# A split-mask attention and maxout FFN kernel: the program rewritten as one list of commands, with the engine of each mask and copy, the place of each FFN unit and the whole order set by an offline search

One core of one Trainium2 chip. The metric is device time in microseconds (us), the median of several executions. One execution of each kernel was also profiled; its span is from the first to the last instruction, some 2 us less than the time.

## The reference

Attention over 4 batches of 8 heads, 768 positions of 64 values, then a feed-forward layer (FFN) with three input weights and a maximum in place of an activation. Cut to what matters:

```python
causal = rel >= 0
stream_keep = causal & (is_sink | in_win)            # 4 sinks, a window of 64
mask = np.where(retrieval_head, causal, stream_keep) # per head
a = softmax(where(mask, q @ k.T / 8, -1e9))
x = (a @ v) -> (3072, 512)
h = max(max(x @ w1, x @ w2), x @ w3)                 # 512 -> 768
return h @ w_out                                     # 768 -> 512, float32
```

## The kernel before

Attention goes in 16 tiles `t`: batch, half of the positions, four heads. A tile's scores are made in two or four units `u`; ScalarE (ACT) takes the exponential of a unit from PSUM into `pt`; a mask multiplies part of `pt` in place; TensorE (PE) multiplies it with v (`av`); VectorE (DVE) divides by the row sums, giving `x`. When all of a half batch's `x` is turned, its FFN block is queued: 18 units of four products, then three output tiles of six products. FFN units fill PE's time between score units. In the timelines shown below DVE starts its instructions in the order of the program, so that one which waits holds up those behind it (run e4 further down has 19.2 us of such waiting).

The order comes out of a table: each row has the number of FFN units beside one score unit and four strings of other commands. Masks and copies follow fixed rules.

```python
MASK_ON_DVE = ((2, 0, 1), (3, 0, 0), (3, 0, 1), (3, 1, 3), (5, 0, 0), ...)   # 10 instructions
def masks(t, i, u):                      # right behind the scores of (t, u)
    ...
    engine = nc.vector if (t, i, u) in MASK_ON_DVE else nc.gpsimd
    engine.tensor_tensor(out=x, in0=x, in1=m, op=ALU.mult)
# in ffn():
    if wi == 0:
        acc[ni] = accp.tile([P, HALF], FP16, tag="acc", name="acc")
        nc.scalar.copy(out=acc[ni], in_=yy[:, 0:HALF])        # always ACT
    else:
        nc.vector.tensor_tensor(out=dst, in0=yy[:, 0:HALF], in1=acc[ni], op=ALU.max)
    yield
...
PROGRAM = (
    (2.4, True, "", "", "cast 1 2 dp", ""),        # 2.4 FFN units beside scores (2, 0)
    (1.6, True, "", "av 2 0", "", "turn 1 0 0 0"),
    ...
```

The softmax here doesn't subtract the row's maximum and nothing guards it: scores larger than these inputs give would overflow.

Of the kernel before, what the change touches and what calls it, by code (L numbers as in the profile page):

```python
# [38 lines left out]
APART = [(0, 0, 1, (384,), 128, 0), (1, 1, 1, (384,), 128, 0)] + MASKED[1][1:]  # L39

# [11 lines left out]
def kernel(  # L52
# [14 lines left out]
    nc = tc.nc  # L67
# [21 lines left out]
    BY_DMA = (2, 4, 5, 6, 7, 8, 9, 10, 11, 12, 13, 14, 15)  # L89

    consts = ctx.enter_context(tc.tile_pool(name="consts", bufs=1))
    stage = ctx.enter_context(tc.tile_pool(name="stage", bufs=3))
    half16 = ctx.enter_context(tc.tile_pool(name="half16", bufs=3))
# [27 lines left out]
    def load_pairs(half, hp, n, engines, alone=False):  # L121
        for nm, src, eng in zip(("ks", "qs"), (k, q), engines):
            st = stage.tile([P, 4, HB, D], FP32, tag=nm, name=nm)
            m = 2 if alone else 2 * n
            for h in range(0, 2 * n, m):
                eng.dma_start(
                    out=st[:, h : h + m],
                    in_=src[
                        0, 2 * hp + h : 2 * hp + h + m, half * HALF : (half + 1) * HALF
                    ].rearrange("h (p j) d -> p h j d", p=P),  # L130
                )
            for i in range(n):
                staged.setdefault((half, hp + i), []).append(st[:, 2 * i : 2 * i + 2])

# [12 lines left out]
    def turn_pair(half, hp, *engines):  # L147
# [4 lines left out]
        for part, op in enumerate(engines):  # L152
            tr = bank([P, 1024], FP16, "tr")
            for i in range(n):
                for j in range(HB):
                    c = i * HALF + j * P
                    nc.tensor.transpose(  # L157
                        tr[:, c : c + P],
                        xs[part + i][:, j].rearrange("p h d -> p (h d)"),
                        ident,  # L160
                    )
# [34 lines left out]
    after = consts.tile([1, 2], FP16, name="after")  # L196

    def sync_after(x):
        nc.sync.dma_start(out=after, in_=x)
# [3 lines left out]
    def load_v(b, half, engines=None):  # L203
        engines = engines or (nc.sync,) * HB
        vs = stage.tile([P, H, HB, D], FP32, tag="vs", name="vs")
        for j in range(HB):
            r0 = half * HALF + j * P
            engines[j].dma_start(
                out=vs[:, :, j], in_=v[b, :, r0 : r0 + P].rearrange("h p d -> p h d")
            )  # L210
        staged_v[b, half] = vs

    load_pairs(0, 0, 1, (nc.sync, nc.scalar))
    ir32 = consts.tile([1, 2 * H], mybir.dt.int32, name="ir32")
    nc.sync.dma_start(out=ir32, in_=is_retrieval.bitcast(mybir.dt.int32).unsqueeze(0))
    load_pairs(0, 1, 1, (nc.sync, nc.scalar))
    load_pairs(0, 2, 2, (nc.sync, nc.scalar), True)
    load_v(0, 0)


    zero = consts.tile([P, 512], FP16, name="zero")
    nc.vector.memset(zero, 0.0)

# [52 lines left out]
    def head_flags():  # L276
        flags = bank([P, H], FP32, "flags")
        nc.tensor.matmul(flags, base[0:1, 0:P], RT1, start=True, stop=True)
# [26 lines left out]
    def load_weight(wi):  # L305
        if wi < 3:
            nc.gpsimd.dma_start(
                out=w_t[wi],
                in_=(moe_w1, moe_w2, moe_w3)[wi].rearrange("(ks p) n -> p ks n", p=P),
            )  # L310
        else:
            nc.gpsimd.dma_start(
                out=woutt, in_=moe_w_out.rearrange("(ns p) m -> p ns m", p=P)
            )
# [4 lines left out]
    def ffn(b, half):  # L319
# [15 lines left out]
        for wi, ni in order:  # L335
            yy = psum()
            for ks in range(KS):
# [5 lines left out]
                )  # L343
            if wi == 0:
                acc[ni] = accp.tile([P, HALF], FP16, tag="acc", name="acc")
                nc.scalar.copy(out=acc[ni], in_=yy[:, 0:HALF])  # L346
# [6 lines left out]
        for tb in range(HB):  # L353
# [5 lines left out]
            for c, op, eng in (  # L359
                (0, nc.scalar.copy, nc.sync), (n, nc.vector.tensor_copy, nc.scalar),  # L360
# [14 lines left out]
    queue = []  # L375

    def fill(n):
# [28 lines left out]
    def scores(t, u, pairs=(0, 1)):  # L406
# [5 lines left out]
        m = 1 if u == 1 and (t == 0 or t == 1 and pairs == (0,)) else 2  # L412
# [37 lines left out]
        for x, st in sts.items():  # L450
# [5 lines left out]
            if not early:  # L456
                masks(t, i, u)


    MASK_ON_DVE = ((2, 0, 1), (3, 0, 0), (3, 0, 1), (3, 1, 3), (5, 0, 0), (5, 1, 0), (5, 1, 1), (7, 0, 1))  # L460

    def masks(t, i, u):
# [3 lines left out]
        for at, u0, nu, cols, n, m0 in APART if t in (3,) else MASKED[half]:  # L466
# [11 lines left out]
            engine = nc.vector if (t, i, u) in MASK_ON_DVE else nc.gpsimd  # L478
# [4 lines left out]
    def av(t, i):  # L483
# [29 lines left out]
        if t in BY_DMA:  # L513
# [6 lines left out]
    def turn_x(t, i, op=None):  # L520
        b, half, qd = where(t)
        hp = 2 * qd + i
        if t not in BY_DMA:
# [10 lines left out]
        if hp == NHP - 1:  # L534
# [4 lines left out]
    cast_pair(0, 0, (act, act))  # L539
    idle_work(8)  # L540
    read_flags()
    idle_work(2)
    head_flags()
    turn_pair(0, 0, dve, act)
    head_masks(0, True)
    cast_pair(0, 1, (pool, act))
    turn_pair(0, 1, dve)
    cast_pair(0, 2, (pool, pool))
    scores(0, 0, (0,))
    scores(0, 1, (0,))  # L550
    head_masks(1, True)
    load_weight(0)
    scores(0, 0, (1,))
    far_flags()
    cast_pair(0, 3, (pool, pool))
    head_masks(3, True)
    head_masks(2, True)
    turn_pair(0, 2, dve)
    scores(0, 1, (1,))
    turn_pair(0, 3, dve)  # L560
    prep_v(0, 0, dve, nc.gpsimd)
    prep_v(1, 0, dve, nc.vector)
    load_pairs(1, 0, 2, (nc.gpsimd, nc.gpsimd))
    prep_v(1, 1, pool, nc.gpsimd)
    scores(1, 0, (0,))
    scores(1, 1, (0,))
    scores(1, 0, (1,))
    prep_v(0, 1, act, nc.vector)
    av(0, 0)
    scores(1, 1, (1,))  # L570
    av(1, 0)
    av(0, 1)
    turn_x(0, 0, act)
    av(1, 1)
    load_weight(1)
    turn_x(0, 1, act)
    head_masks(0)
    cast_pair(1, 1, (act, act))
    load_pairs(1, 2, 2, (nc.gpsimd, nc.gpsimd))
    load_weight(2)  # L580
    load_v(0, 1, (nc.gpsimd,) * HB)
    turn_x(1, 0, dve)
    turn_x(1, 1, dve)
    cast_pair(1, 0, (act, act))
    fill(4)
    head_masks(2)
    turn_pair(1, 1, dve)
    turn_pair(1, 0, dve)
    head_masks(3)
    load_weight(3)  # L590
    fill(1)
    fill(1)
    fill(1)
    head_masks(1)






    FIRST = 4
    PROGRAM = (
        (2.4, True, "", "", "cast 1 2 dp", ""),
        (2.4, False, "load 1 0", "", "cast 1 3 da", ""),
        (2.0, False, "", "pair 1 2", "load 1 1", ""),
        (2.2, False, "pair 1 3", "v 2 0 ap", "", "v 2 1 ap"),
        (2.2, False, "", "gate, load_v 1 0", "", ""),
        (1.6, True, "", "av 2 0", "", "turn 1 0 0 0"),
        (1.0, True, "turn 1 0 0 1", "", "av 2 1, turn 1 0 1 0", ""),
        (2.2, True, "turn 1 0 1 1, load_v 1 1", "", "v 3 1 pp, v 3 0 ap, x 2 0", "turn 1 1 0 0"),  # L610
        (3.6, False, "turn 1 1 0 1", "x 2 1", "turn 1 1 1 1, av 3 1", ""),
        (2.8, False, "v 4 0 pp, av 3 0", "turn 1 1 1 0", "v 4 1 ap", ""),
        (3.6, False, "x 3 0, x 3 1", "", "", ""),
        (3.6, False, "av 4 0", "", "x 4 0, v 5 1 pp", "x 4 1, v 5 0 ap"),
        (2.8, False, "", "", "av 4 1", "av 5 0, load 2 0, v 6 0 pp"),
        (3.6, False, "x 5 0", "load 2 1", "", "av 5 1"),
        (3.8, False, "", "x 5 1", "", ""),
        (2.8, False, "", "load_v 2 0", "turn 2 0 1 0", "v 6 1 ap"),
        (4.8, False, "turn 2 0 0 1", "", "turn 2 0 0 0", "av 6 0"),
        (4.2, False, "", "", "", "x 6 0, x 6 1, turn 2 0 1 1"),  # L620
        (3.4, False, "", "av 6 1", "turn 2 1 0 1", ""),
        (5.4, False, "load_v 2 1", "v 7 0 ap, turn 2 1 0 0", "turn 2 1 1 0", "v 7 1 ap"),
        (3.4, False, "", "turn 2 1 1 1", "v 8 0 ap, x 7 0", "av 7 0"),
        (3.8, False, "av 7 1", "", "", "v 8 1 pp"),
        (3.94, False, "x 7 1", "", "av 8 0", "v 9 0 ap, av 8 1"),
        (3.2, False, "", "x 8 0, x 8 1", "", ""),
        (3.94, False, "", "", "av 9 0, v 9 1 ap", "load 3 0"),
        (3.6, False, "", "x 9 0, load 3 1", "x 9 1", ""),
        (5.6, False, "v 10 0 ap, av 9 1", "v 10 1 ap", "", ""),
        (3.14, False, "", "load_v 3 0", "turn 3 0 1 0", ""),  # L630
        (3.6, False, "turn 3 0 0 1", "av 10 0", "turn 3 0 0 0", ""),
        (3.4, False, "", "x 10 0", "av 10 1", "turn 3 0 1 1"),
        (6.2, False, "", "", "turn 3 1 0 1", "v 11 0 ap"),
        (3.2, False, "load_v 3 1", "turn 3 1 0 0", "turn 3 1 1 0", ""),
        (3.2, False, "v 11 1 pp", "x 10 1, turn 3 1 1 1", "v 12 0 ap", "av 11 0, x 11 0"),
        (3.4, False, "", "av 11 1", "", "v 12 1 ap"),
        (5.0, False, "x 11 1", "", "av 12 0", "v 13 0 ap, av 12 1"),
        (3.2, False, "", "x 12 0, x 12 1", "", ""),
        (4.0, False, "", "", "av 13 0, v 13 1 pp", ""),
        (5.2, False, "", "x 13 0", "x 13 1", ""),  # L640
# [86 lines left out]
```

## Time and profile before

| | before |
|---|---|
| time, median of 3 runs | 200.88 us (200.74 to 201.45) |
| span, mean TensorE clock | 199.3 us, 0.998 |
| busy: PE, DVE, ACT, POOL (GpSimd) | 95%, 61%, 66%, 62% |
| PE waits of over 0.1 us | 5.5 us, the last at 49.5 us |
| first FFN product, second block's first | 17.79 us, 50.08 us |

Here PE's share, 95% against 66% for the next, says what sets the time, and the place of its waits says where time can be won. Waits here and below are the gaps ahead of an instruction in the timeline of the engine, each with the instruction that ended it.

### The profile page before, as it was taken

The page shows a single profiled execution, that of the slowest core. Times are in us where ns is not written, and L with a number is a line of the kernel's source. Part 1 is how long each engine was busy: PE and PEld are TensorE (multiplying, and loading weights), DVE is VectorE, ACT ScalarE, POOL GpSimd, SP SyncE. Part 2 cuts the span into 40 slices and gives each one's busy share as a digit, 9 for nine tenths or more (in the row PEclk, how much of TensorE's full clock was granted, in tenths as well). Part 3 has the DMA queues.
Part 4 walks back from the last instruction along what each step waited for, and adds up shares of the span by engine and source line. Part 5 has one row for each costly group of instructions (what it writes and reads, how often), then busy time and mean ns, then how long its engine had stood idle before and what let it go on. Part 6 is the DMA issues. An engine that isn't in the chain of part 4 may idle for free.

```text
span 199.3 us, 5133 instructions
## 1 busy us (share of the span) xinstructions
PE 189.7 (95%) x2059; PEld 109.5 (55%) x2059; DVE 122.5 (61%) x241; ACT 131.7 (66%) x206; POOL 123.3 (62%) x154
## 2 busy tenths in 40 slices
PE   7897999996999999999999999999999999999992
PEld 2455555545566465574555565565555565755652
DVE  2698587999687829861555649961555234543540
ACT  4585798786966776676786775848758769323221
POOL 3599159789887906787969635799847447400000
PEclk9999999999999999999999999999999999999999
DMA  6999999994949991904359995513410250023004
GB/s 182 270 213 245 278 238 212 213 202 112 256 81 154 194 274 43 178 0 146 95 101 132 170 254 141 85 26 98 116 23 20 105 76 20 3 64 135 3 0 158
DMA packets 43245, 26.48 MB, mean 133 GB/s; under 512 B 33558, under 2 KB 38230, under 8 KB 43222
## 3 DMA queue, kind: packets, MB, share of 16 engines
q1 hardware_dynamic: 37206, 15.01, 34.9%
q0 software_dynamic: 4784, 10.23, 26.7%
q10 hardware_dynamic: 1232, 0.92, 1.5%
q8 instruction: 16, 0.26, 0.6%
q14 instruction: 7, 0.06, 0.1%
HBM read 25.17 MB, written 6.29 MB: 158 GB/s over the span
## 4 chain that ended last, share of the span: by engine, by line
PE 78%; DVE 8%; ACT 4%; DMA 3%; issue 3%; POOL 2%; SPq 1%; ACTq 0%; POOLq 0%; DVEq 0%
PE yy L338 43%; PE yy L364 12%; PE st L441 10%; PE oacc L495 8%; DVE KQ L190 4%; PE yst L338 3%; ACT pt L452 3%; DMA ks<-in_k_dram 2%; DVE x L505 2%; DMA out_dram<-ot 1%; PE tr L157 1%; PE yst L364 1%; POOL kn L139 1%; DVE hT L349 1%; POOL qn L139 0%
## 5 line engine op out<-in xcount | busy, mean ns | idle before, releaser
L479 POOL TENSOR_TENSOR pt<-pt,mk 128x512 f16<-128x512 f16 (+1 forms) x76 | 80.6, 1084 | 34.8 <-ACT pt L452 34.7
L452 ACT ACTIVATE pt<-st 128x1024 f16<-128x1024 f32 (+3 forms) x99 | 83.1, 894 | 19.4 <-PE st L441 18.6
L349 DVE TENSOR_TENSOR acc<-yy,acc 128x384 f16<-128x384 f32 x45 | 25.1, 558 | 28.9 <-PE yy L338 19.3
L338 PE MATMUL yy<-xT,w1t 128*128 128x384 f16 x180 | 36.1, 327 | 0.1
L338 PE MATMUL yy<-xT,w0t 128*128 128x384 f16 x180 | 35.6, 326 | 0.4 <-DVE xT L531 0.4
L338 PE MATMUL yy<-xT,w2t 128*128 128x384 f16 x180 | 35.7, 327 | 0.0
L346 ACT CAST acc<-yy 128x384 f16<-128x384 f32 x45 | 21.0, 485 | 17.0 <-PE yy L338 10.5
L364 PE MATMUL yy<-woutt,hT 128*128 128x512 f16 (+1 forms) x138 | 32.0, 375 | 0.0
L441 PE MATMUL st<-KQ 32*128 32x384 f16 (+4 forms) x560 | 28.7, 279 | 1.0 <-DVE KQ L190 0.8
L349 DVE TENSOR_TENSOR hT<-yy,acc 128x384 f16<-128x384 f32 x45 | 25.1, 560 | 6.6 <-PE yy L338 4.0
L495 PEld LDWEIGHTS <-pt 128*128 128x128 f16 x672 | 24.0, 97 | 5.3 <-issue 2.1
L190 DVE STREAM_TRANSPOSE KQ<-kq 128x384 f32<-128x384 f32 x24 | 25.7, 1130 | 0.0
L338 PEld LDWEIGHTS <-w0t 128*128 128x128 f16 x192 | 18.2, 98 | 12.9 <-issue 1.0
L495 PE MATMUL oacc<-va,pt 128*128 128x65 f16 x352 | 24.8, 193 | 0.3 <-ACT va L392 0.3
L338 PEld LDWEIGHTS <-w2t 128*128 128x128 f16 x192 | 17.6, 98 | 13.3 <-issue 2.1
L338 PEld LDWEIGHTS <-w1t 128*128 128x128 f16 x192 | 17.2, 98 | 12.8 <-issue 1.3
L370 ACT COPY ot<-yy 128x512 f32<-128x512 f32 x22 | 12.9, 588 | 15.9 <-PE yy L364 9.6
L364 PEld LDWEIGHTS <-hT 128*128 128x128 f16 x150 | 14.0, 98 | 14.6 <-issue 0.3
L441 PEld LDWEIGHTS <-KQ 32*128 32x128 f16 (+1 forms) x560 | 12.2, 93 | 17.8 <-issue 11.5
L495 PE MATMUL oacc<-vf,pt 128*128 128x65 f16 x320 | 21.2, 193 | 0.8 <-POOL vf L394 0.8
L505 DVE TENSOR_TENSOR x<-oacc,rc 128x384 f16<-128x384 f32 x32 | 17.8, 557 | 1.1
L503 DVE RECIPROCAL rc<-oacc 128x6 f32<-128x6 f32 x32 | 6.1, 192 | 20.0 <-PE oacc L495 19.8
(70 smaller groups left out, 129.9 us busy)
## 6 DMA issues: line engine op xcount, KB each, us to landing
out_dram<-ot SPq DMA_DIRECT2D x23, 256.0 KB, 3.1
vs<-in_v_dram SPq DMA_DIRECT2D x21, 256.0 KB, 6.3
kq<-in_k_dram POOLq DMA_DIRECT2D x6, 384.0 KB, 5.6
kq<-in_q_dram POOLq DMA_DIRECT2D x6, 384.0 KB, 8.0
qs<-in_q_dram ACTq DMA_DIRECT2D x4, 192.0 KB, 4.0
ks<-in_k_dram SPq DMA_DIRECT2D x4, 192.0 KB, 3.6
w0t<-in_moe_w_dram POOLq DMA_DIRECT2D x1, 768.0 KB, 7.4
ks<-in_k_dram POOLq DMA_DIRECT2D x2, 384.0 KB, 7.2
```

Source lines behind the costliest of these rows:

```text
L190: nc.vector.transpose(out=dst.rearrange("c (p j) -> c j p", j=n)[:, j0:j1], in_=src.rearrange("c (j i) -> c j i", i=R),)
L338: nc.tensor.matmul(yy[:, 0:HALF], w_t[wi][:, ks, ni * P : (ni + 1) * P], xT[b, half][ks].rearrange("p a t -> p (a t)"), start=(ks == 0), s ...
L346: nc.scalar.copy(out=acc[ni], in_=yy[:, 0:HALF])
L349: nc.vector.tensor_tensor(out=dst, in0=yy[:, 0:HALF], in1=acc[ni], op=ALU.max)
L364: nc.tensor.matmul(yo[:, 0:n], hT[ns][:, tb * P : (tb + 1) * P], woutt[:, ns, c : c + n], start=(ns == 0), stop=(ns == NNB - 1),)
L370: op(out=ot[:, c : c + n], in_=yo[:, 0:n])
L441: nc.tensor.matmul(sts[g // m][:, g % m, c0 : c0 + n * P], KQ[rows, 0, ki * P : (ki + 1) * P], KQ[rows, 1, t0 : t0 + n * P], start=(c0 == ...
L452: nc.scalar.activation(out=pts[t, i][:, u, h0 : h0 + m, 0:w], in_=st[:, :, 0:w], func=AF.Exp, scale=sc,)
L479: engine.tensor_tensor(out=x, in0=x, in1=m, op=ALU.mult)
L495: nc.tensor.matmul(o[:, qi, hl, 0 : D + 1], pt[:, u, hl, c : c + P], vv[:, 2 * hp + hl, ki, 0 : D + 1], start=(idx == 0), stop=(idx == len ...
L503: nc.vector.reciprocal(out=rc, in_=o[:, :, :, D])
L505: nc.vector.tensor_tensor(out=x, in0=o[:, :, :, 0:D], in1=rc.unsqueeze(3).to_broadcast([P, HB, 2, D]), op=ALU.mult,)
```

## The change

The table and the rules are replaced by one list of commands, run from left to right. Each mask (`k tile pair unit engine`), FFN unit (`f 1 engine`, the engine being that of its copy out of PSUM), cast and turn is an entry. An offline search set the order and engines. The intent is to remove the waits that rules and a table cannot avoid. The commands used here: `s` scores and exponential, `k` mask, `v` prepares v, `av` product with v and division (with `D` a DMA turns the result), `x` turns a result on PE, `turn` turns q or k on DVE, `cast`/`turnp` do so for the first batch, `load*`, `ld` and `w` issue loads; the rest build masks and flags. Engines: `a` ACT, `d` DVE, `p` POOL.

```diff
-    MASK_ON_DVE = ((2, 0, 1), (3, 0, 0), ...)
-    def masks(t, i, u):
+    def masks(t, i, u, engine):
-                nc.scalar.copy(out=acc[ni], in_=yy[:, 0:HALF])
+                copy_out[0](out=acc[ni], in_=yy[:, 0:HALF])
-    def fill(n):
+    def fill(n, op=nc.scalar.copy):
+        copy_out[0] = op
-    PROGRAM = ((2.4, True, "", "", "cast 1 2 dp", ""), ...)   # 47 rows, and the calls ahead of it
+PROGRAM = (
+    "cast 0 1 ap, idle 8, cast 0 0 aa, cast 0 2 pp, read, idle 2, w 0, flags, em 0, em 2, em 1",
     ... (cut)
+    "x 0 1 d, av 1 0, x 1 0 d, cast 1 1 pa, w 2, x 1 1 a, turnp 1 1 ad, f 1 d, f 1 a, f 1 a",
     ...
+    "v 8 0 pp, f 1 a, f 1 a, av 7 0 D, k 8 0 0 d, k 7 1 1 d, av 7 1 D, x 7 1 d, f 1 d, f 1 a",
     ...
+    "k 10 0 1 p, load 3 1, f 1 a, load_v 3 0, f 1 a, k 10 0 3 p, turn 3 0 0 1, av 10 0 D",
     ...
+    "f 1 a, v 11 1 pp, av 11 1 D, f 1 a, k 12 0 0 d, f 1 a, v 12 0 pp, s 12 1, turn 3 1 1 1",
+    "x 11 1 a, v 12 1 ad, k 12 1 0 d, turn 3 1 1 0, s 13 0, k 13 0 0 p, f 1 d, k 12 0 1 d",
     ...
+    for line in PROGRAM:
+        for item in line.split(", "):
+            name, *args = item.split()
+            do[name](*args)
```

Loads got options that the list hardly uses, and the product that spreads the head flags reads a row of ones of its own.

## The prediction

> **What bounds the kernel now.** I read the busy shares first, then the PE work in stretches, then the waits, the chain, and the groups for durations.
>
> ```profile
> PE 189.7 (95%) x2059; PEld 109.5 (55%) x2059; DVE 122.5 (61%) x241; ACT 131.7 (66%) x206; POOL 123.3 (62%) x154
> DMA  6999999994949991904359995513410250023004
> ```
> TensorE is busy for 95% of the span and nothing else passes 66%, so only 9.6 us of it are idle by this count. The second line shows the DMA engines full for the first 50 us (ten slices of 5 us).
>
> ```profile
> 0.00:10.00 10.00, 7.95 (x43) 3.58 (x43) 4.81 (x20) 4.60 (x9) 4.50 (x15) 1.00 0.93 226
> 10.00:20.00 10.00, 8.62 (x114) 5.43 (x111) 9.29 (x23) 7.14 (x15) 10.00 (x17) 1.00 1.12 229
> 20.00:30.00 10.00, 9.88 (x83) 5.42 (x81) 7.33 (x15) 8.59 (x15) 3.68 (x7) 1.00 1.10 257
> 30.00:40.00 10.00, 9.92 (x122) 5.72 (x120) 8.88 (x14) 8.18 (x11) 8.39 (x10) 1.00 1.14 213
> 40.00:50.00 10.00, 7.79 (x131) 4.52 (x127) 9.76 (x17) 7.53 (x12) 9.61 (x11) 1.00 0.70 155
> 50.00:60.00 10.00, 10.00 (x132) 6.07 (x121) 7.52 (x15) 8.01 (x14) 8.26 (x13) 1.00 0.80 171
> 60.00:80.00 20.00, 20.00 (x233) 11.38 (x232) 14.23 (x25) 14.19 (x20) 12.12 (x12) 1.00 0.94 167
> ```
> Columns: PE, PEld, DVE, ACT, POOL. All idle PE time lies before 50 us and in the tail after the last matmul (about 195.7 to 199.3). From 50 us PE stays full although no other engine is. In 40 to 50 DVE (9.76) and POOL (9.61) are full while PE drops to 7.79.
>
> The chain of waits says why:
> ```profile
> 39.32 1.99 DVE KQ L190 x2
> 41.37 0.56 DVE x L505
> 41.92 1.99 DVE KQ L190 x2
> 43.92 0.25 DVE pt L479
> 44.17 2.94 DVE KQ L190 x3
> ```
> DVE turns the next batch's q and k, eight transposes of about 1 us, before batch 1 can score; the first feed-forward block is used up meanwhile, and the next one's first product runs at 50.08.
>
> **PE work without stalls.** I summed starts to starts, not busy time. From stretches of the chain: four 384-wide products 0.65 us (32 in 5.31), six 512-wide 1.29 (12 in 2.59), 16 score matmuls 0.56, 8 in 0.34 to 0.45, attention-value 0.37 (12) or 0.97 (30), three transposes 0.17. Over the whole program this gives 176 us from the first transpose (5.75) to the last matmul (195.7), 190 us apart: about 14 us of stalls and rounding, some 10 of them before 50.08, where only 34.3 us of work is done in 44.3. After 50 the stalls that I can find add to under 1 us. **So what can be won lies before 50 us, and about 10 us is its ceiling.**
>
> [...]
> - [...] one 384-wide product is drawn as 327 ns but 32 take 5.31 us, 166 ns each. Hence the sums above.
> - [...]
> - [...] the smaller mask on DVE is slower in the mean (1096 ns) than the larger (588 ns), and one lasted 2.31 us.
> - [...]
>
> ```profile
> L479 DVE TENSOR_TENSOR pt<-pt,mk 128x256 f16<-128x256 f16 x4 | 4.4, 1096 | 0.8 <-ACT pt L452 0.8
> L479 DVE TENSOR_TENSOR pt<-pt,mk 128x512 f16<-128x512 f16 x6 | 3.5, 588 | 3.0 <-ACT pt L452 3.0
> L479 POOL TENSOR_TENSOR pt<-pt,mk 128x512 f16<-128x512 f16 x64 | 73.1, 1160 | 34.7 <-ACT pt L452 34.7
> L346 ACT CAST acc<-yy 128x384 f16<-128x384 f32 x45 | 21.0, 485 | 17.0 <-PE yy L338 10.5
> L392 ACT CAST va<-vs 128x384 f16<-128x384 f32 x22 | 11.3, 516 | 0.0
> ```
>
> **The change part by part.** Comparing the order of instructions:
> - PE gets 3 more transposes (one more x pair turned on PE, one fewer by DMA): +0.17 us. Nothing else is added or removed on it.
> - ACT loses 17 acc copies (485 ns), 5 output copies (588), 11 v casts (516) and 3 q/k casts (510), and gains 4 copies of turned q/k and one of x (480 to 800): 8.2 + 2.9 + 5.7 + 1.5 - 2.7 = 15.6 us less, to about 116.
> - DVE takes those 17 (an estimate of 0.56 each, as its 384-wide PSUM operations take) and 5 (0.69, extrapolated from 0.42 for 256 and 0.56 for 384), 8 of the v casts (0.45), 2 q/k casts (0.54), 3 more vf products, and 31 masks instead of 10. The masks cost 0.3 to 0.4 us alone and 0.6 to 1.1 beside POOL. That is 9.5 + 3.5 + 3.6 + 1.1 + 1.6 + 6 to 20, less 2 for copies given to ACT: 23 to 37 us more, to some 145 to 160.
> - POOL loses 21 masks (0.7 to 1.16 us) and gains 3 v casts: about 20 us less, to 103.
>
> Total work is thus not the point, since PE has the same; **the placing is**. I split the new list at the second block's first product and added each engine's work with the durations above, operations back to back, masks on DVE uncontended.
>
> Up to the first product the list holds 7.6 us of PE work. It starts later: ACT casts pair 1's k first, whose load landed only at 5.6 before, so both of pair 0's inputs are ready near 6.9 instead of 5.2 (transposes began at 5.75). The exponentials then end near 16.6 (15.9 before). The fourth x copy stands behind a q cast on ACT that waits for the second half's q; before, ACT's cast of it ended a DMA wait at 19.36. So the first block's first four-matmul product finishes near 19.9, against 19 before. The second weight is now issued behind another 0.79 MB of q and k; at the roughly 250 GB/s that the profile's slices show here this is 3 us, from 23.4 to 25 or 26. PE has its six first-weight products to run till about 25, so this costs little beyond them.
>
> From there to the second block's first product: PE 22.1 us, DVE about 20.5, ACT about 20. Saturated, that product comes at 25.2 + 22.1 = 47.3, against 50.1. With three engines at over 90% and each waiting in order for the others, I add 1 to 2 us: **48.3 to 49.3, a win of 1 to 2 us.**
>
> The next 20.8 us of PE work, which ran without stalls before, now carry 18.7 us of DVE work plus contended masks (seven or so, 0.5 us each, an estimate from the rows above): DVE at about its limit. Loss 0 to 1.5 us.
>
> From there PE has 120.5 us of work and DVE 77: PE bound, as before; the tail is unchanged.
> Sum: 200.88 - 1.5 + 0.7 = 200.1 by my hand sums, 195 if the stalls before 50 us go as the search intended.
>
> **The rivals.**
> 1. *The search works.* It could place every operation and may know landing times better than I do; if the second weight lands by 23.4 and the following work saturates PE, the second block starts at about 45.5 and nothing is lost after: a win of 4.5, to 196.4; with an earlier first product too, 194.5. For it: 10 us of stalls are there, and that DVE and POOL are full from 40 to 50 is just what a finer order can spread. Against: DMA is full for those 50 us.
> 2. *DVE becomes the bound.* With 23 to 37 us more on it, masks slowed by POOL hold up the maxima behind them, and PE waits between 25 and 70 us. Then 200 to 203. For it: the 2.31 us mask. Against: DVE averaged 61%.
> 3. *The prologue waits for loads.* The reordered loads hold the first and second weights' products 2 us longer, nothing wins it back: 200 to 202.
>
> **Range and chances.** A search of all this freedom is seldom spent for nothing, so I weight rival 1 and my hand sum about equally and set 198.0, 80% within 194.3 to 201.4. Over 2% faster means below 196.9: 0.38. Over 2% slower means above 204.9: 0.04. Within: 0.58.
>
> **What would show it.** Right: the second block's first product near 47 to 49 us instead of 50.08; DVE above 72% of the span, ACT below 60%, POOL near 52%; no PE wait after 70 us; PE work unchanged. For rival 1: that product before 46.5 and PE full from 25 us. For rival 2: DVE over 9 in each ten us from 25 to 70, masks on DVE above 0.8 us in the mean, PE waiting for DVE maxima or copies of it. For rival 3: PE idle near 17 to 26 us, released by a weight's DMA or by the ACT copy of x. I am wrong outright if PE stalls after 70 us, or if the first products start well before 18 us.

(Cut from it are remarks that no trace or run of this case shows. No term of its sum is cut: 200.88 - 1.5 + 0.7 = 200.1 stands, and 198.0 is that weighed about equally with rival 1. The author's figures for masks on DVE, 0.3 to 0.4 us alone and 0.6 to 1.1 beside POOL, are rough: in the trace of before the three with POOL idle took 0.28 to 0.43 us, the five with POOL busy throughout 0.46 to 2.31.)

## The result, and the profile after

The changed kernel is correct and **slower by 10%**: 221.9 us (median of 4 runs, 219.59 to 223.15) against 200.91. One of the 4 runs (223.15, clock 0.959) is slow; the fast ones took 219.59 to 222.35. The ratio is 1.0988, 95% interval 1.0923 to 1.1053. Here and below a ratio is that of fast runs alone, so not quite the ratio of the medians quoted, and gains between runs are taken from it, with 1% as 2.0 us: by it the loss is 20 us. The before kernel ran beside every experiment, at 200.86 to 201.42.

From the page of the changed kernel, busy totals and the slices of 5.5 us:

```profile
PE 196.0 (89%) x2062; PEld 111.5 (51%) x2062; DVE 146.0 (66%) x298; ACT 118.6 (54%) x176; POOL 100.7 (46%) x134
...
PE   7695969869799899969999699958999999999993
...
PEclk9889999999999999999999969995899999999999
```

The work moved just as counted beforehand (DVE 146.0, ACT 118.6, POOL 100.7), and PE has three instructions more. But PE's row now has holes up to 155 us, and **the granted TensorE clock, full up to the last microseconds before, drops to 0.50 near 10, 130 and 150 us**.

The stretches that answer to those of before; columns are stretch, length, PE, PEld, DVE, ACT, POOL busy (instructions), clock, DMA share, GB/s:

```profile
10.00:20.00 10.00, 8.30 (x94) 5.06 (x93) 7.66 (x21) 7.34 (x16) 7.48 (x14) 0.87 1.07 250
...
40.00:50.00 10.00, 7.24 (x105) 4.20 (x108) 7.64 (x14) 7.70 (x10) 8.18 (x10) 1.00 0.26 50
50.00:60.00 10.00, 8.44 (x130) 5.10 (x119) 6.81 (x12) 6.28 (x9) 7.02 (x11) 1.00 0.99 238
60.00:80.00 20.00, 18.89 (x207) 10.23 (x205) 19.02 (x37) 12.83 (x19) 10.29 (x14) 1.00 0.67 115
...
120.00:140.00 20.00, 18.09 (x188) 9.46 (x187) 12.38 (x23) 11.53 (x16) 10.45 (x11) 0.91 0.61 132
140.00:160.00 20.00, 16.55 (x163) 8.68 (x162) 11.59 (x24) 7.33 (x12) 5.50 (x8) 0.83 0.11 32
```

From 40 to 50 us *no* engine is full, where DVE and POOL were full before. From 140 to 160 PE works 16.55 of 20 us at a clock of 0.83, and the other engines idle too. Each waits for another, as the timelines below show for one place: a low busy share (DVE's is 11.59 of these 20 us, and it holds PE up for 3.45) does not say that an engine is not in the way.

PE's waits of over 0.1 us add to 20.2 us, 14.7 more than before. Half clock (0.50 granted) adds to that: by the clock of each stretch below full, 8 to 12.5 us lost 1.65 us, 128.1 to 132.1 1.7, 150 to 158 3.0, together 6.4, where before lost 0.4 in all. 14.7 + 6.0 = 20.7, and the spans differ by 220.6 - 199.3 = 21.3. **So in these two profiled executions they hold nearly the whole loss.** The share of the half clock varies between executions of the same program: the fast runs had mean clocks of 0.969 (the profiled one), 0.977 and 0.984, and took 222.35, 221.45 and 219.59 us. The second block's first product comes at 58.09, 8.0 us later than before; the rest is lost behind it. The waits of a microsecond and more behind that point:

| at us | wait | ended by | what the list does there |
|---|---|---|---|
| 76.8 | 1.04 | DVE, the last maximum of a block | a turn and a mask (1.11 us, POOL busy beside it) stand ahead of it on DVE |
| 98.4 | 1.76 | DVE mask `k 7 1 1 d` | stands behind the division of `av 7 0` and the masks of `k 8 0 0 d`, just ahead of its own `av 7 1` |
| 127.1 | 1.75 | POOL mask `k 10 0 3 p` | stands behind the two issues of `load 3 1` |
| 150.0 | 3.45 | DVE turns | two turns of 1.12 us just ahead of `s 13 0`, no FFN unit between |

The last one in the timelines of PE, then DVE (start, us, what, idle before and its end):

```profile
146.15 0.40 PE L550 MATMUL st<-KQ 32*128 32x256 f16 x8
150.01 1.04 PE L550 MATMUL st<-KQ 32*128 32x384 f16 x16 [3.45 <-DVE KQ L264]
150.98 1.46 PE L435 MATMUL yy<-xT,w0t 128*128 128x384 f16 x4
```

```profile
146.69 0.55 DVE L455 TENSOR_TENSOR hT<-yy,acc 128x384 f16<-128x384 f32 x1
147.15 1.12 DVE L264 STREAM_TRANSPOSE KQ<-kq 128x384 f32<-128x384 f32 x1
148.07 0.33 DVE L503 TENSOR_TENSOR vf<-vs,far 128x128 f16<-128x128 f32 x1
148.32 0.59 DVE L583 TENSOR_TENSOR pt<-pt,mk 128x512 f16<-128x512 f16 x2
148.84 1.12 DVE L264 STREAM_TRANSPOSE KQ<-kq 128x384 f32<-128x384 f32 x1
```

PE runs out of work at 146.5. DVE turns, prepares v, masks and turns again, until 150.0; `s 13 0` needs both turns. Then the same score matmuls take 1.04 us, not 0.63, and the products start 1.26 to 1.28 us apart where they took 0.65. The clock in these stretches, columns as above:

```profile
126.00:128.10 2.10, 1.02 (x31) 0.97 (x35) 1.05 (x2) 0.35 (x1) 1.02 (x1) 1.00 0.90 120
128.10:132.10 4.00, 4.00 (x26) 1.56 (x27) 0.76 (x2) 2.52 (x3) 0.00 (x0) 0.57 1.03 213
...
150.00:155.20 5.20, 5.19 (x29) 2.33 (x30) 1.92 (x4) 1.94 (x2) 1.96 (x2) 0.50 0.00 0
```

At a granted clock of 0.50 PE is drawn full, 5.19 of 5.20 us, while its products start 1.26 to 1.28 us apart instead of 0.65: about half the work. Read in steps of 0.1 us, the clock is at half from 9.2 to 12.6 and from 128.65 to 132.05, 3.4 us each, and from 149.15 to 156.0, 6.8 us. So half clock stands behind the 3.45 us wait, but it fell at 149.15, 2.6 us after PE had run dry and before that wait ended at 150.0, and it also fell behind the 1.75 us wait; in b1 below it stands behind a wait of 0.98 us. The wait of 1.76 us at 98 us has full clock behind it (1.00 from 98.4 to 104); and the 1.75 us wait stands in the traces of h1, r1 and r2 below too (1.73 to 1.76), each time with full clock behind it. So half clock is not a fixed price of such a wait; what decides was not settled.

### The profile page after: what moved, and what is told of

Its sections match the earlier page's. It is cut to its first block, busy times and chain, and to the rows that moved or that the text cites. A ratio compares the mean times of both kernels' runs of the same rounds, so it can differ in the third digit from the quotient of the medians.

```text
span 220.6 us, 5132 instructions
## 1 busy us (share of the span) xinstructions
PE 196.0 (89%) x2062; PEld 111.5 (51%) x2062; DVE 146.0 (66%) x298; ACT 118.6 (54%) x176; POOL 100.7 (46%) x134
## 4 chain that ended last, share of the span: by engine, by line
PE 72%; DVE 13%; ACT 5%; POOL 3%; DMA 3%; issue 2%; SPq 0%; DVEq 0%; ACTq 0%; POOLq 0%
PE yy L435 38%; PE yy L471 11%; PE st L550 9%; PE oacc L599 8%; DVE KQ L264 3%; ACT pt L561 3%; DVE pt L583 3%; PE yst L435 3%; DVE x L609 2%; POOL pt L583 2%; DMA ks<-in_k_dram 2%; DVE hT L455 1%; PE tr L228 1%; DMA out_dram<-ot 1%; DVE rc L607 1%
## 5 line engine op out<-in xcount | busy, mean ns | idle before, releaser
L583 POOL TENSOR_TENSOR pt<-pt,mk 128x512 f16<-128x512 f16 (+1 forms) x55 | 58.4, 1078 | 44.2 <-ACT pt L561 37.6
L550 PE MATMUL st<-KQ 32*128 32x384 f16 (+4 forms) x560 | 29.3, 284 | 8.3 <-DVE KQ L264 5.7
L435 PE MATMUL yy<-xT,w2t 128*128 128x384 f16 x180 | 36.5, 331 | 0.0
L435 PE MATMUL yy<-xT,w0t 128*128 128x384 f16 x180 | 36.5, 334 | 0.0
L471 PE MATMUL yy<-woutt,hT 128*128 128x512 f16 (+1 forms) x138 | 33.7, 390 | 1.2 <-DVE hT L455 1.2
L503 POOL TENSOR_TENSOR vf<-va,far 128x384 f16<-128x384 f16 x15 | 12.4, 827 | 33.4 <-DVE pt L583 14.9
L550 PEld LDWEIGHTS <-KQ 32*128 32x128 f16 (+1 forms) x560 | 12.2, 94 | 25.7 <-issue 13.6
L435 PEld LDWEIGHTS <-w1t 128*128 128x128 f16 x192 | 17.9, 99 | 12.2 <-issue 1.3
L471 PEld LDWEIGHTS <-hT 128*128 128x128 f16 x150 | 14.5, 100 | 18.3 <-issue 2.5
L477 ACT COPY ot<-yy 128x512 f32<-128x512 f32 x17 | 10.0, 587 | 23.0 <-PE yy L471 20.5
L452 ACT CAST acc<-yy 128x384 f16<-128x384 f32 x28 | 13.4, 483 | 12.8 <-PE yy L435 8.3
```

The costliest lines, as they stand in the source:

```text
L435: nc.tensor.matmul(yy[:, 0:HALF], w_t[wi][:, ks, ni * P : (ni + 1) * P], xT[b, half][ks].rearrange("p a t -> p (a t)"), start=(ks == 0), s ...
L452: copy_out[0](out=acc[ni], in_=yy[:, 0:HALF])
L471: nc.tensor.matmul(yo[:, 0:n], hT[ns][:, tb * P : (tb + 1) * P], woutt[:, ns, c : c + n], start=(ns == 0), stop=(ns == NNB - 1),)
L477: op(out=ot[:, c : c + n], in_=yo[:, 0:n])
L503: vf_engine.tensor_tensor(out=vf[j][:, hs, k0:k1, 0:D], in0=vs[:, hs, 0:1] if half == 0 else va[j][:, hs, k0:k1, 0:D], in1=far[:, hs, k0:k ...
L550: nc.tensor.matmul(sts[g // m][:, g % m, c0 : c0 + n * P], KQ[rows, 0, ki * P : (ki + 1) * P], KQ[rows, 1, t0 : t0 + n * P], start=(c0 == ...
```

## The experiments

The first question was whether the order, the engines or the frame costs the time; then which commands. I wrote the old order out as a list for the new program and mixed the two. In runs with another list the profile's line numbers are 9 higher (masks L592, turns L273, maxima L464; up to 15 in r2). All results were correct, and of these runs all are fast but two of e2's four. Times are medians of 4 runs (5 or 6 for s1 and b1, b2).

### c0: the old order and engines in the new program

```diff
-    "cast 0 1 ap, idle 8, cast 0 0 aa, cast 0 2 pp, ...   (new list)
+    "cast 0 0 aa, idle 8, read, idle 2, flags, turnp 0 0 da, ...   (old order, old engines)
```

> Control: the list interpreter of the changed kernel fed with the old order and the old engines (its instructions per engine are the old kernel's, in the old order; the flags matmul reads a separate row of ones, and the early q/k staging has buffers of its own). If order and engines are all that matters, 200.9 us, ratio 1.00 within 0.5%. If the new frame itself (other buffers, the row of ones) costs something, more than 202.

Measured: 201.32 us, ratio 1.0006 (0.9953 to 1.0058). The frame costs nothing; the list alone is to be explained.

### e1 and e2: each kernel's order with the other's engines

```diff
 e1: old order                       e2: new order
-    f 1 a, k 6 1 2 p, v 5 1 pp, ...    -    k 6 1 2 d, f 1 d, v 5 1 ap, ...
+    f 1 d, k 6 1 2 d, v 5 1 ap, ...    +    k 6 1 2 p, f 1 a, v 5 1 pp, ...
```

> The old order with the new engine for every mask, v preparation, feed-forward copy, q/k cast and turned-q/k copy. Theory ORDER (the sequence puts operations that wait for each other next to each other with no feed-forward work between, so PE runs dry): 201 to 204. Theory ENGINES (24 us more work on DVE make it the bound): 210 or more, most of the 21 us lost.

> The new order with the old engine for the same operations. Theory ORDER: stays above 214, near 218. Theory ENGINES: comes back to 205 or less. If both matter and add, this and the run before lose together about 21 us.

Measured: e1 214.98 us, ratio 1.069 (1.063 to 1.075), PE waits of 15.0 us. e2 235.47 us (two of the four runs slow), ratio 1.160 (1.147 to 1.173), waits of 28.5 us; both theories for e2 had it too low. The largest item of e2's waits (engine, line, waited for: us in total, times, longest):

```profile
PE oacc L608 <- POOL pt L592: 11.1, 8, 4.3
```

Both parts are harmful by themselves, and they do not add. The new order suits its own engines: with the masks back on POOL it is worse still, and PE's longest waits there are for masks that POOL has late.

### e3 and e4: only the FFN's copies, only the masks

Old order; e3 takes the new engines for the FFN's copies (22 go to DVE), e4 for the masks (31 instead of 10 on DVE).

```diff
 e3: -  f 1 a        e4: -  k 6 1 2 p
     +  f 1 d            +  k 6 1 2 d
```

> The old order; only the 22 feed-forward copies out of PSUM that the new list gives to DVE go there (17 of 384, 5 of 512 columns). Old order with all new engines lost 14 us. If the copies are the cause (a PSUM copy behind a busy DVE holds a bank and the maxima after it): 207 to 212. If the masks are: 201 to 203.

> The old order; only the masks change engine, 31 on DVE instead of 10 (at the places where the old list has them, right after the exponential). If masks are the cause, by standing in DVE's queue until ACT has made the exponential (17.6 us of such idle in the run with all new engines): 207 to 212. If the copies are: 200 to 203. I expect the masks to carry most of the 14 us.

Measured: e3 201.95 us, ratio 1.0023 (0.9985 to 1.0060); e4 210.56 us, ratio 1.0447 (1.0399 to 1.0496). **The copies cost nothing that can be told from noise, and the masks cost 9 of e1's 14 us.** The other 4 or 5, those of the engines of casts, turns and v, I did not take apart. Is it the masks' own time? In e4 they take 0.545 us in the mean. With the new mask engines DVE stands ahead of masks, waiting for an exponential, as the waits of c0 and of e4 show:

```profile
DVE pt L592 <- ACT pt L570: 3.8, 5, 1.4
```

```profile
DVE pt L592 <- ACT pt L570: 19.2, 19, 2.6
```

A mask that comes right behind its scores waits for ACT; on DVE the maxima, turns and divisions stand behind it, and PE behind them. That it is this waiting which costs the time was a guess until m1.

### m1: the same masks on DVE, later in the queue

e4's list, with each of the 23 masks new to DVE moved behind up to two more FFN units, never behind its `av`.

```diff
-    s 6 2, k 6 0 2 d, k 6 1 2 d, x 5 1 d, f 1 a, f 1 a, f 1 a, s 6 3
+    s 6 2, x 5 1 d, f 1 a, f 1 a, k 6 1 2 d, k 6 0 2 d, f 1 a, s 6 3
```

> The old order with the new engines of masks (31 on DVE, 210.6 us), with each of the 23 masks that were newly put on DVE moved up to two FFN units later in the list, never behind the product that reads it; same masks, same engines. Theory (the loss was DVE's queue standing behind masks that wait for ACT's exponential, so that the maxima behind them come late): 201 to 204 us, DVE's wait of masks for the exponential from 19.2 us down to below 8. Rival (DVE loses by the masks' own time, 23 more of 0.5 us, or by contention with POOL, wherever they stand): 208 us or more.

Measured: 203.21 us, ratio 1.0105 (1.0069 to 1.0141), so by the ratios 7 of e4's 9 us came back. DVE's wait for the exponential is c0's again:

```profile
DVE pt L592 <- ACT pt L570: 3.5, 5, 1.4
```

The theory holds and the rival (the masks' work or contention) falls: as many masks on the same engine cost about 2 us where they don't block. This is a finding about the old order. In the changed kernel itself no DVE mask waits for an exponential: its mask groups, shown in the next part, have 0.0 us of idle time ahead of them. The new order had already moved its masks back; e4's loss is not part of its 20 us.

### h1 and h2: one half of the list each

h1 is the old order up to the second block's first product and the new list behind it; h2 is the reverse.

```diff
 h1: -  (new list up to x 3 1)        h2: -  (new list behind x 3 1)
     +  (old order up to there)           +  (old order behind it)
```

> The old list up to the point where the second feed-forward block becomes ready (before: 50 us, after: 58 us), then the new one. From the traces 8 of the 21 us are lost before that point and 13 after it, so 200.9 + 13 = about 214 if the two stages are independent; near 201 if the late stalls only follow from the early ones; near 222 if the lost start is made good later anyway.

> The new list up to the turn of tile 3's second result (just ahead of the second block's first product), then the old order with the old engines. Theory (the losses of the start and of the rest are independent and add): the first block's product starts 8 us late as in the changed kernel and nothing is lost later, so 209 to 212 us, TensorE idle about 13 us in all and none over 0.6 us after 60 us. Rival (DVE or a late load carries the delay on, or a start that ends later leaves more work to overlap and wins some back): outside that, below 207 or above 214 us.

Measured: h1 210.89 us, ratio 1.0474 (1.0413 to 1.0535); h2 209.96, ratio 1.0467 (1.0416 to 1.0518). The rest costs some 9.5 us (I had expected 13) and the start 9.4; the sum, 19, is close to the whole 20. In h1 the same late waits stand (1.04, 1.76, 1.73, 3.45), with half clock behind the last alone: 3.4 us of it, from 141.4, which is 1.4 us after the wait's end. In h2 PE waits 12.2 us, all before 61 us, and never behind it. So the two losses add, and **a loss of the start is not won back**: PE was already full behind it.

### r1 and r2: the 3.45 us wait, in the changed kernel

r1 moves the two turns earlier. r2 leaves the wait, and has PE multiply zeros into a bank that nobody reads meanwhile, to see what the half clock costs by itself.

```diff
 r1: -  s 12 1, turn 3 1 1 1, ..., turn 3 1 1 0, s 13 0
     +  turn 3 1 0 1, turn 3 1 1 1, ..., turn 3 1 0 0, turn 3 1 1 0, ..., s 13 0
 r2: +  warm 14          (14 products of zeros of 128x512, between s 12 1 and s 13 0)
```

> The new list with two DVE transposes moved up (the q half of batch 3's second quad, to right behind its k half, some 15 places earlier on DVE; their data landed long before). It takes away the largest single wait, 3.45 us of PE at 146.6 to 150.0, and the half clock from 149.6 to 155.9 that follows it, 3 us by the products' spacing. Expected 221.9 - 6.5 = 215.5. If the wait only moves elsewhere: 219 or more.

> The new list with 14 matmuls of zeros (3 us) on PE inside that same wait, so the wait stays but PE isn't idle in it. If the 6 us of half clock behind it come from the idle time, they go: products of 0.65 us instead of 1.28 there, 221.9 - 3 = 219. If the clock has another cause: unchanged, 221 to 223.

Measured: r1 217.4 us, ratio 1.0809 (1.0746 to 1.0871); r2 220.98, ratio 1.0978 (1.0924 to 1.1032). PE's timeline of r1 and then of r2:

```profile
146.02 1.11 PE L559 MATMUL st<-KQ 32*128 32x384 f16 x16 [0.69 <-ACT pt L570]
147.07 0.82 PE L444 MATMUL yy<-xT,w0t 128*128 128x384 f16 x4
147.73 0.81 PE L444 MATMUL yy<-xT,w1t 128*128 128x384 f16 x4
```

```profile
146.40 3.19 PE L397 MATMUL sink<-zero 128*128 128x512 f16 x14
149.92 0.63 PE L565 MATMUL st<-KQ 32*128 32x384 f16 x16 [0.33 <-DVE KQ L274]
150.49 0.82 PE L450 MATMUL yy<-xT,w0t 128*128 128x384 f16 x4
151.15 0.81 PE L450 MATMUL yy<-xT,w1t 128*128 128x384 f16 x4
```

From the start of the last scores of tile 12 to the product behind the next output tiles, the changed kernel takes 13.55 us, r1 9.24, r2 11.56. So placing two commands gave 4.3 us at the site, more than the wait itself. In the whole it gave 3.6 us by the ratios, where I had expected 6.5; the other half clock stretches differ between the two traces too (r1 has none near 128, and 3.4 us of it from 20.0). With PE kept busy the scores take 0.63 and the products start 0.66 apart again, which is 2.0 us at the site. Half clock stands at this place in both traces that leave PE idle (the changed kernel, h1) and in neither that does not (r1, r2). **That this wait brings the half clock is thus well supported**, by one trace each. The whole time does not show it: r2 was to take 219, and its ratio differs from the changed kernel's by 0.001, 0.2 us, well inside the intervals. Its profiled execution waited 2.3 us for the first load's cast, where the changed kernel's waited 1.3, and had half clock twice in the first 25 us (7.9 to 11.3 and 21.5 to 24.9).

### h3: the old start, and the rest with seven commands moved

```diff
 (on h1)
-  s 6 2, ..., av 5 1 D, turn 2 0 1 0, f 1 a, k 6 1 2 d, s 6 3, f 1 d
+  s 6 2, ..., av 5 1 D, f 1 a, s 6 3, f 1 d, k 6 1 2 d, turn 2 0 1 0
-  av 7 0 D, k 8 0 0 d, k 7 1 1 d, av 7 1 D
+  k 7 1 1 d, av 7 0 D, k 8 0 0 d, av 7 1 D
-  av 10 0 D, s 11 1, f 1 a
+  s 11 1, f 1 a, av 10 0 D
   (the turns as in r1)
-  s 13 0, k 13 0 0 p, f 1 d
+  f 1 d, s 13 0, k 13 0 0 p
```

> The run with the old start and the new rest (210.9 us), with its five late waits taken out by moving nine commands and changing no engine: the turns of pair 3 1 earlier, one mask ahead of the product whose result DVE would divide first, one product behind the next scores so that the POOL mask behind two load issues is done, a turn and a mask behind the last hT, one FFN unit ahead of the scores of tile 13. Theory (the waits of 1.04, 1.76, 1.73 and 3.45 us and the half clock behind two of them are the whole loss of the rest): 210.9 minus 8.0 of waits minus 2.5 of half clock minus some left = 200 to 203 us, clock 1.00. Rival (the order of the rest is slow in many small places, and waits taken out reappear elsewhere): 205 us or more.

(It says nine commands; the list has seven.) Measured: 202.43 us, ratio 1.0057 (1.0017 to 1.0097). Of h1's 9.5 us, 8.4 are gone. The page's slices of PE and of its clock:

```profile
PE   7897899996999999999999899999999999999992
...
PEclk9999999999999999999999999999999999999999
```

So these few placements were most of the loss of the rest (together; only the turns were also moved alone), and DVE at 71% of the span in this run is no bound.

### s1 and r3: the start with seven commands moved, and all repairs in the changed kernel

```diff
-  cast 0 1 ap, idle 8, cast 0 0 aa            +  cast 0 0 aa, cast 0 1 ap, idle 8
-  av 0 1, x 0 1 d, av 1 0, x 1 0 d, ..., x 1 1 a
+  av 0 1, av 1 0, x 0 1 d, x 1 1 a, x 1 0 d
-  cast 1 0 dd, turnp 1 0 dd, f 1 d            +  cast 1 0 dd, f 1 d, turnp 1 0 dd
-  s 2 0 0, s 2 1, f 1 a                       +  s 2 0 0, f 1 a, s 2 1
-  f 1 a, s 3 0, s 3 1 1                       +  s 3 0, f 1 a, s 3 1 1
-  x 2 0 d, s 3 3 0, k 3 0 2 p, av 2 1 D       +  s 3 3 0, k 3 0 2 p, av 2 1 D, x 2 0 d
```
s1 has these on h2 (old rest), r3 has these and h3's on the changed kernel.

> The run with the new start and the old rest (209.96 us), with nine commands of the start moved and no engine changed: the first pair's casts ahead of the second's, two turns of results one product later, a cast one FFN unit ahead of its turn, one FFN unit between two score units in two places, one turn of a result behind the next product. Theory (the start loses by placement): of its waits 0.88, 0.88, 1.11, 0.90, 0.90, 0.88 us most go, so 4 to 5 us less: 205 to 206 us. Rival (DVE's own work, near full from 20 to 60 us, or the loads bound the start, and the waits come back elsewhere): 208 us or more.

> The changed kernel with the moves of the repaired start and of the repaired rest together: the same commands on the same engines, only the order differs. Theory (placements add): the repaired start's run plus the 1.3 us that the repaired rest still has over the old rest, 206 to 208 us against 221.9, clock 0.99 or more. Rival (repairs of the start push waits into the rest): 211 us or more.

Measured: s1 206.33 us, ratio 1.0261 (1.0223 to 1.0299); r3 207.63, ratio 1.0334 (1.0291 to 1.0376). (Here too the moves are seven, not nine.) By the ratios some 4 us of the start's 9 came back, at the edge of what I had expected (205 to 206). The waits of 0.90 and of 0.88 us went or shrank but for one, and the one for a cast grew from 1.11 to 1.71. **Fourteen moves took 13 of the changed kernel's 20 us away**, with the same commands on the same engines. What is left of the start's loss, about 5 us, was not settled in full; r3's trace has waits of 1.40 and 0.96 us for DVE turns in it, at 46.7 and 54.6 us, which I did not repair.

### b1 and b2: a try to beat both

The old order with three moves where before still waits, between 45 and 50 us; b2 then also puts two copies on ACT.

```diff
 b1: -  s 3 3 1, ..., v 3 1 pp, v 3 0 ap       +  k 3 1 1 p, v 3 1 pp, ...
     -  turn 1 1 1 1, av 3 1, ..., av 3 0      +  av 3 1, ..., av 3 0, ..., turn 1 1 1 1
     -  x 3 0 d, x 3 1 d, s 5 0                +  x 3 0 d, x 3 1 d, f 1 a, f 1 a, s 5 0
 b2: -  v 4 1 ap, x 3 0 d, x 3 1 d             +  x 3 0 a, x 3 1 a, v 4 1 ap
```

> A try to beat both: the old order and engines with three moves between 37 and 52 us: tile 3's second value half cast and masked on POOL in an idle 1.8 us instead of just ahead of the product that waits 0.75 us for it; one DVE turn behind the division that TensorE waits 0.63 us for; two FFN units ahead of the scores that wait 0.53 us for the last turn. Expectation: 1.0 to 1.5 us less than the kernel before, 199.4 to 200.2 us, the waits at 45.5, 48.5 and 49.5 gone or halved. Rival (DVE bound from 39 to 50 us, so the waits move elsewhere): 200.6 to 201.2 us.

> The try b1 (202.27 us) with the two copies of tile 3's turned results on ACT instead of DVE, where they stood behind two turns, and ACT's value cast behind them. Theory (the 0.98 us wait and the half clock after it cost b1 its gain): 2.0 us less, 200.0 to 200.8 us, no half clock. Rival (DVE bound from 39 to 50 us): 201.5 us or more.

Measured: b1 202.27 us, ratio 1.0073 (1.0040 to 1.0106); b2 201.05, ratio 1.0001 (0.9968 to 1.0033). b1 was to gain 1.0 to 1.5 us and lost as much. In its profiled execution the copies stood behind two turns on DVE: a new wait of 0.98 us, and half clock behind it. The stretch from 50 to 52 us of b1 and of b2, columns as above:

```profile
50.00:52.00 2.00, 2.00 (x10) 0.72 (x13) 0.15 (x1) 0.58 (x2) 2.00 (x3) 0.59 1.30 241
```

```profile
50.00:52.00 2.00, 1.94 (x22) 1.19 (x21) 0.91 (x1) 1.96 (x3) 2.00 (x3) 1.00 1.24 277
```

The half clock is not the whole of it: b1's runs with mean clocks of 0.996 to 1.0 still took 201.6 to 202.3. b2 mended the wait and gained 1.4 us over b1, but only drew level with the kernel before, although its PE waits add to 4.5 us against 5.5. No version here beats before.

## Why the prediction was wrong

The time fell outside the range (194.3 to 201.4) and on the side that I had given 4%.

**What held.** The amounts: ACT "to about 116" (118.6), DVE "145 to 160" (146.0), POOL "103" (100.7), PE's work unchanged. The 21 masks more on DVE were to add "6 to 20" us: by the groups of the changed kernel all 31 took 17.5, against 7.9 for the 10 before.

```profile
L583 DVE TENSOR_TENSOR pt<-pt,mk 128x512 f16<-128x512 f16 x26 | 15.7, 608 | 0.0
...
L583 DVE TENSOR_TENSOR pt<-pt,mk 128x256 f16<-128x256 f16 x5 | 1.8, 359 | 0.0
```

That at most 10 us were to be won, before 50 us, was not contradicted: b2 took a microsecond of waits away there and won nothing that could be measured. (One slip of reading did not matter: the DMA row's tenth digit is 4, so the DMA engines were full for some 45 us, not 50.)

**The step that failed first: "operations back to back".** I took the largest of the engines' sums of work up to the second block's first product for the bound and added "1 to 2 us" for three engines that wait in order for one another: 48.3 to 49.3. It came at 58.09. The first product was late already: it began at 22.22 against 17.79 and took some 0.65 us, so that it ended near 22.9, where I had forecast 19.9. Two 0.88 us waits for a result's division, the 1.34 us wait for the first cast and 1.65 us of half clock (8 to 12.5 us) lie ahead of it. The rest are waits for turns, casts and the exponentials of two score units one behind the other. h2 put the whole of it at 9 us, and s1 showed 4 of them to be placement alone; what the other 5 are was not settled. Sums of work bound a stage from below; in an order where a command stands right behind what it needs, they say little about it.

**The step that failed next: "From there PE has 120.5 us of work and DVE 77: PE bound, as before".** The page of before showed PE full from 50 us, and I took that for a property of the work. It was one of the old order, which had FFN units between a command and its use. The new one loses 9.5 us there (h1), and seven moves give 8.4 of them back (h3). I had written that I would be wrong outright if PE stalled after 70 us; it stalls four times.

**The rival closest to it had the right engine and the wrong mechanism.** "DVE becomes the bound", through masks slowed by POOL. It would have shown as masks of over 0.8 us; the 31 took 0.56 in the mean, the wide ones 0.61. (Beside POOL they do take longer: in the changed kernel's trace the 13 wide masks with POOL idle took 0.40 to 0.46 us each, the 10 with POOL busy throughout 0.47 to 1.50. It is not what costs the time: m1 took some 7 us less than e4 with as much DVE work, 129.9 us busy against 129.4.) Masks on DVE can do harm (e4, 9 us, in the old order), by standing in DVE's queue while ACT has not finished (m1 gave 7 us back with as many masks). In the changed kernel they do so by what stands ahead of them or behind: the mask of the 98.4 us wait stands behind a division, the maximum of the 76.8 us wait behind a turn and a mask. DVE's timeline above, from 146.69 to 150 us, has its instructions in the order of the list; had I held each DVE command against when its input is ready and what waits behind it, I would have seen these places. The other two rivals, a search that works and a late load, did not come about: the 1.3 us wait for the first cast is the only one of over a microsecond that could lie with a load.

**A term that was missing: the clock.** I had no entry for a PE that waits and then runs at half clock; it is about 6 of the 21.3 us between the profiled executions, and by the mean clocks less in the other fast runs.

**A weight that was wrong.** "A search of all this freedom is seldom spent for nothing." That a search had been made told me nothing about what it measured by, and I let it raise the chance of a gain to 38%. What it took for the time is not known, so that it left out the queues or the clock stays a guess.

## What to carry to other kernels

When work moves to an engine that others wait for, ask of each moved instruction what it waits for and what stands behind it in that queue, not only how long it takes. A full engine in the profile before is full under that order; a new order has to be looked through for every place where a command stands right behind the one that feeds it, for there one wait can cost twice, once as idle time and, in some executions, once as half clock (here 3.45 us of wait, and 3.0 us lost at half clock from 150 to 158). Before a searched order is kept or thrown away, list its waits of over a microsecond: four of them, with the half clock behind one or two, were half the loss here, and moving seven commands took most of that away.
